# Attention by four heads a step with the softmax weights as the stationary operand, mixing in plain float32, and 1024 instead of 768 inner columns in the first part

## The chip, the cores and the metric

The kernel runs on one core of a Trainium2 chip. The metric is the device time of one execution in microseconds; the time of a kernel is the median of several executions. TensorE (PE) multiplies, with its weight loads (PEld) shown apart; VectorE (DVE), ScalarE (ACT) and GpSimd (POOL) do elementwise work; SyncE (SP) issues most DMAs.

## The reference

Three blocks follow each other on 4 batches of 576 tokens. The first is windowed attention with 8 heads of 64; the second takes the real part of a two-dimensional Fourier transform of its output, adds it, and runs a dense MLP of 2048 inner columns on the normalised sum; the third sends each token to one of 8 experts of 1024 inner columns.

```python
scores = q @ k.T / sqrt(D) - slope[h] * |i - j|      # kept where 0 <= i - j < 128
attn = softmax(scores);  x = attn @ v                # (B, S, H*D)
u = x + real(fft(fft(x, axis=seq), axis=model))
un = (u - mean) / sqrt(var + 1e-6)
y = u + relu(un @ w_ch1) @ w_ch2                     # 512 -> 2048 -> 512
# experts: e = argmax of the gate (or the token before's); out = p[e] * relu(y @ w1[e]) @ w2[e]
```

## The kernel before, in words

All large matrix products are done in the reduced float32 format of TensorE with each operand split in a high and a low part, so that one product is three matmuls (`mm3`, lines 168 to 170). Plain float32 operands give two matmul records for each matmul of the program.

The program has a first part, in which attention, mixing (the Fourier transform) and the first 768 inner columns of the MLP run interleaved; a second part, which runs the other 1280 inner columns and routes tokens; and the experts. `FA` is the number of inner columns of the first part, `CB = 256` those of a chunk of weights. In both parts the MLP runs over 9 groups of 256 tokens, and for each group over the chunks; a chunk is two inner steps of 128 columns. A step (`ffn`, line 572) is 12 matmuls into `hps` (256 moving columns) and 6 into `acc` (512 moving columns), with one ACT and one DVE pass over `hps` between them. The partial sums of the first part go to `pd` in DRAM and the second part adds to them. MLP weights come as 64-bit words and are converted on the core (`convert`: one load of 256 KB, two ACT, three DVE and one POOL instruction for each of 8 pieces of a chunk).

Attention works on units of two heads and one tile of 128 queries: 20 units for each batch, the last tile of each pair of heads 64 rows. `scores` multiplies queries and keys into PSUM (two heads on two halves of the 64-deep rows), DVE folds the two key blocks into one by a mask (`copy_predicated`) and adds the bias with a row minimum in one instruction (line 345); `exps` takes the exponential with row sums on ACT; `flip` transposes the weights on TensorE (`pt`), copies them to SBUF and separates the two key blocks with two masks on POOL; `values` has v stationary (64 columns, two heads side by side) and the weights moving, so that its result `x` comes out transposed, one column per query. `reciprocals` transposes the row sums, and `natural`, at the start of the mixing of a batch, transposes the result back to one row per query (`xps`) and multiplies by the reciprocals.

The mixing of a batch (`mixing`) folds rows, splits them (`zi`), transforms along the sequence (`zps`, five PSUM tiles), splits again, transforms along the model axis (`pc`, `pz`) and adds the result to x. There are two buffers for x, so `natural` stores it to DRAM (`xd`) and `again` loads it back for the final addition. The sum goes to `ud` in DRAM, and the normalisation of the MLP loads it from there.

Generators for attention, mixing, conversion and MLP are put into lanes with start and length in abstract units (`ATT`, `MIX`, `CONV_`, `MLP_`); the lane with the lowest position is advanced next. A scheduler of the framework then reorders within its own view of durations, so that each engine's queue is a fixed list; every engine and SP's DMA queue work through it strictly in order. The weights of the second part take the memory of the first part's attention and mixing tiles, and so are converted when these are finished.

Of the kernel before, what the change touches and what calls it, by code (L numbers as in the profile page):

```python
# [30 lines left out]
K1 = HALF + 2  # L31
K2 = DM // 2 + 2
# [6 lines left out]
FA = 768  # L39
WB = 4  # L40
GB_ = 3
PB_ = 0
RB = 2
UB = 2
MB = 4
SETUP = 6.5
WARM = 24
ATT = ((0, 25), (25, 25), (50, 24), (75, 25))
MIX = ((25, 12), (50, 11), (77, 12), (101.5, 9))
CONV_ = (30, 14)  # L50
MLP_ = (40.0, 130)
XB = 2
QR = 4
VB = 3
TB_ = 4
FL = 2
EY = 10
VL = 4
PHB = 2
LI = 1  # L60
NP = 5

# [38 lines left out]
def split12(a):  # L101
    a = np.ascontiguousarray(a, dtype=np.float32)
    bits = a.view(np.uint32).astype(np.uint64)
    hi = ((bits + 0x7FF + ((bits >> 12) & 1)) & 0xFFFFF000).astype(np.uint32).view(np.float32)
    return hi, (a - hi).astype(np.float32)


def constants():
# [13 lines left out]
    c["tab1"] = np.ascontiguousarray(np.stack(split12(tab1), 1))  # L122
    c["tab2"] = np.ascontiguousarray(np.stack(split12(tab2), 1))
# [4 lines left out]
    slopes = -8.0 * 2.0 ** (-8.0 * (np.arange(H, dtype=np.float32) + 1) / H)  # L128
    rel = np.where(k <= q, q - k, q - k + P).astype(np.float32)
    bias = (slopes[:, None, None] * rel[None]).astype(np.float32).transpose(1, 0, 2)  # L130
    c["bias"] = np.ascontiguousarray(bias).astype(ml_dtypes.bfloat16)
# [25 lines left out]
def build(ctx, tc, a, out):  # L157
# [39 lines left out]
    xd = {(b, k): dram.tile([P, 2, DM], F32, name=f"xd{b}{k}") for b in range(B) for k in range(3)}  # L197
# [10 lines left out]
    ps_p = ctx.enter_context(pool("ps_p", PB_, space=PSUM)) if PB_ else ps_g  # L208
# [45 lines left out]
    qk = c1.enter_context(pool("qk", QR))  # L254
    sm = c1.enter_context(pool("sm", 3))
    ps_x = c1.enter_context(pool("ps_x", 2, space=PSUM))

    tab1 = cst.tile([P, 2, 2, 3, K1], F32R, name="tab1")
    tab2 = cst.tile([P, 2, 2, 2, K2], F32R, name="tab2")
    alt = cst.tile([1, K2], F32R, name="alt")  # L260

# [7 lines left out]
    def load_heads(b, hp):  # L269

        r = [qk.tile([P, S], F32, tag="raw", name=x) for x in ("qr", "kr")]
        for t, x in zip(r, ("q", "k")):
            nc.sync.dma_start(out=t, in_=a[x][b, hp])
        vr = sm.tile([P, NB, P], F32, tag="vr", name="vr", bufs=VB)
        last["load"] = nc.sync.dma_start(out=vr, in_=a["v"][b, hp])
        return r[0], r[1], vr

    raw0 = load_heads(0, 0)

    z16 = slab([P, 4 * P], BF16, "z16", "w", WB)  # L280
# [11 lines left out]
    bias = cst.tile([P, H, P], BF16, name="bias")  # L292
    nc.sync.dma_start(out=bias, in_=a["bias"])
    id16 = cst.tile([P, P], BF16, name="id16")
    nc.sync.dma_start(out=id16, in_=a["id16"])
    rec = {}
    mixed = [-1]

    def attention(b, ot):

        sums = sm.tile([P, NB, H], F32, tag="sums", name="sums", bufs=2)
        units = [(hp, i) for hp in range(4) for i in range(NB)]
        W, T, X, R, M = {}, {}, {}, {}, {}

        def rows(i):
            return P if i < 4 else D

        def scores(us):

            if b == 0:  # L310
                ss = [ps_a.tile([P, 2, 2 * P], F32, tag=f"acc{h}", name="s") for h in range(2)]
            else:
                ss = [ps_g.tile([P, 2, 2 * P], F32, tag="g", name="s") for h in range(2)]
            for u in us:

                T[u] = sm.tile([P, 2, P], F32, tag="t", name="t", bufs=TB_)
                M[u] = sm.tile([P, 2], F32, tag="mx", name="mx", bufs=TB_)
            c0s = [P, 0, 0, 0, 0]
            whole = all(0 < units[u][1] < 4 for u in us)
            for x, u in enumerate(us):  # L320
                hp, i = units[u]
                m = rows(i)
                qr, kr, _ = R[hp]
                w = m if i == 0 else P + m
                c0 = P if i == 0 else 0
                o = [s[0:m, x, c0:c0 + w] for s in ss]
                qc = slice(i * P, i * P + m)
                ks = slice(max(i - 1, 0) * P, max(i - 1, 0) * P + w)
                if i == 0:
                    for h in range(2):  # L330
                        nc.tensor.matmul(o[h], lhsT=id16, rhs=first, start=True, stop=False)

                for h in range(2):
                    r = slice(h * D, h * D + D)
                    nc.tensor.matmul(o[h], lhsT=qr[r, qc], rhs=kr[r, ks], start=i > 0, stop=True)  # L335
            for h in range(2):
                s = ss[h]
                if whole:
                    nc.vector.copy_predicated(s[:, :, 0:P], mask.unsqueeze(1).to_broadcast([P, 2, P]), s[:, :, P:])
                for x, u in enumerate(us):  # L340
                    hp, i = units[u]
                    m = rows(i)
                    if i > 0 and not whole:
                        nc.vector.copy_predicated(s[0:m, x, 0:m], mask[0:m, 0:m], s[0:m, x, P:P + m])
                    nc.vector.tensor_tensor_reduce(out=T[u][0:m, h], in0=s[0:m, x, c0s[i]:c0s[i] + P], in1=bias[0:m, 2 * hp + h], scale=SC,  # L345
                                                   scalar=3.0e38, op0=ALU.add, op1=ALU.min, accum_out=M[u][0:m, h:h + 1])

        def exps(u):
            hp, i = units[u]
            m = rows(i)  # L350
            t, mx = T[u], M.pop(u)
            for h in range(2):
                e = 2 * hp + h
                nc.scalar.activation(t[0:m, h], t[0:m, h], AF.Exp, bias=mx[0:m, h:h + 1], scale=-1.0, accum_out=sums[0:m, i, e:e + 1])  # L354

        def reciprocals():

            s1 = ps_g.tile([E, 4 * P], F32, tag="g", name="s1")
            s2 = ps_g.tile([E, D], F32, tag="g", name="s2")
            for i in range(4):  # L360
                nc.tensor.transpose(s1[:, i * P:(i + 1) * P], sums[:, i, :], ident)
            nc.tensor.transpose(s2, sums[0:D, 4, :], ident[0:D, 0:D])
            srow = sm.tile([E, S + 1], F32, tag="tmp", name="srow", bufs=1)
            nc.gpsimd.memset(srow[:, S:S + 1], 1.0)
            nc.scalar.copy(srow[:, 0:HALF + 1], s1[:, 0:HALF + 1])
            nc.vector.tensor_copy(srow[:, HALF + 1:HALF + 1 + D], s2[:, ::-1])
            nc.vector.tensor_copy(srow[:, HALF + 1 + D:S], s1[:, 4 * P - 1:HALF:-1])
            pt = ps_g.tile([P, 6, E], F32, tag="g", name="rt")
            r = sm.tile([P, 6, E], F32, tag="rec", name="rec", bufs=2)
            for kt in range(3):  # L370
                for ab in range(2):
                    c, n = kt * P + ab * HALF, P if kt < 2 else 33
                    nc.tensor.transpose(pt[0:n, 2 * kt + ab], srow[:, c:c + n], ident[0:E, 0:E])
            for x, n in ((slice(0, 4), P), (slice(4, 6), 33)):
                nc.vector.tensor_scalar_add(r[0:n, x], pt[0:n, x], 1.0e-9)
                nc.vector.reciprocal(r[0:n, x], r[0:n, x])
            rec[b] = r

        def flip(u):
            hp, i = units[u]  # L380
            m = rows(i)
            t = T.pop(u)
            pt = ps_p.tile([P, 2, P], F32, tag="g", name="pt")
            for h in range(2):
                nc.tensor.transpose(pt[:, h, 0:m], t[0:m, h, :], ident[0:m, 0:m])
            ph = sm.tile([P, 2, P], F32, tag="ph", name="ph", bufs=PHB)
            nc.scalar.copy(ph[:, :, 0:m], pt[:, :, 0:m])
            W[u] = slab([P, 2, 2 * P], F32, "w", "w", WB)
            if i > 0:
                nc.gpsimd.affine_select(out=W[u - 1][:, :, P:P + m], in_=ph[:, :, 0:m], pattern=[[0, 2], [-1, m]],  # L390
                                        compare_op=ALU.is_gt, fill=0.0, base=0, channel_multiplier=1)
            last["pool"] = nc.gpsimd.affine_select(out=W[u][0:m, :, 0:m], in_=ph[0:m, :, 0:m], pattern=[[0, 2], [1, m]],
                                                   compare_op=ALU.is_ge, fill=0.0, base=0, channel_multiplier=-1)

        def values(u):
            hp, j = units[u]
            vr = R[hp][2]
            w = W.pop(u)
            if j == 0:
                X["x"] = ps_x.tile([P, 4 * P], F32, tag="x", name="x")  # L400
                X["b"] = ps_p.tile([P, D], F32, tag="g", name="ob")
            n = rows(j)
            q0, q1 = max(j * P, D), min((j + 2) * P, S)

            if j == 0:

# [777 lines left out]
```

## Time and profile before

| | us |
|---|---|
| median of 3 runs | 1089.79 (1087.11 to 1098.1) |
| profiled execution | 1080.29 |
| its span, first to last instruction | 1078.6 |
| PE busy, as a union of records | 986.9 (92%) |
| DVE, ACT, POOL busy | 565.0, 402.1, 218.3 |
| mean granted TensorE clock, as a share of 2.4 GHz | 0.929 |

The profiled execution stands 9.5 us under the median of the runs. Busy time of PE holds pipelined records that overlap, so the distance between starts of neighbouring records, not their length, is what one costs. A row of the timeline gives start, length, engine, line, operation, tiles, shapes and the number of merged records, and in brackets the idle time of the engine before it with what ended it. In the table of stretches PEclk is the share of full clock that TensorE was granted.

### The profile page before, as it was taken

How to read it: one execution, taken by the hardware profiler on the slowest of the kernel's cores; microseconds unless marked ns; L12 is line 12 of the kernel's file. 1: busy time of each engine (PE TensorE's matmuls, PEld its weight loads, DVE VectorE, ACT ScalarE, POOL GpSimd, SP SyncE). 2: the span in 40 equal slices, each digit the busy share in tenths (PEclk: the TensorE clock that was granted, in tenths of full speed). 3: DMA queues.
4: the chain of work that ended last, by engine and by line, in shares of the span. 5: the costliest groups of instructions: out<-in, count | busy, mean ns of one | idle time of the engine just before them, and what ended most of it. 6: DMA issues, size and time to landing. Idle time of an engine off the chain costs nothing. (4 is left out here: it accounts for less than half of the span.)

```text
span 1078.6 us, 17056 instructions
## 1 busy us (share of the span) xinstructions
PE 986.9 (92%) x5857; PEld 788.8 (73%) x5857; DVE 565.0 (52%) x1835; ACT 402.1 (37%) x1102; POOL 218.3 (20%) x321
## 2 busy tenths in 40 slices
PE   8989669989979879989999999998997999999994
PEld 4456346657657767768888888887786998888993
DVE  4686577457554647864333425343666744455510
ACT  5544444444423324543111111111425644545520
POOL 2513321122111002342111212112212222111100
PEclk9766689989989889999999999999997999999997
DMA  7742553335231346683444313441428855454400
GB/s 225 269 147 86 161 167 110 113 99 174 86 99 41 121 127 195 188 243 98 98 98 99 67 49 82 98 98 55 152 60 266 279 192 176 149 189 160 146 18 18
DMA packets 128509, 142.92 MB, mean 133 GB/s; under 512 B 17668, under 2 KB 89604, under 8 KB 128092
## 3 DMA queue, kind: packets, MB, share of 16 engines
q1 hardware_dynamic: 105244, 119.17, 35.1%
q0 software_dynamic: 23168, 22.56, 8.9%
q8 instruction: 48, 0.79, 0.3%
q14 instruction: 49, 0.40, 0.1%
HBM read 108.62 MB, written 35.96 MB: 134 GB/s over the span
## 5 line engine op out<-in xcount | busy, mean ns | idle before, releaser
L582 ACT ACTIVATE h<-hps 128x256 fp32r<-128x256 f32 x152 | 58.0, 382 | 249.7 <-PE hps L170 249.5
L583 DVE SCALAR_TENSOR_TENSOR h<-hps,h 128x256 fp32r<-128x256 f32 x152 | 63.8, 420 | 149.5 <-ACT h L582 149.3
L168 PE MATMUL acc<-t,h 128*128 128x512 f32 x304 | 127.8, 420 | 10.1 <-ACT h L582 10.1
L165 DVE TENSOR_TENSOR t<-we,t 128x512 fp32r<-128x512 f32 x144 | 95.1, 693 | 64.8 <-ACT t L164 61.6
L169 PE MATMUL acc<-t,h 128*128 128x512 f32 x304 | 121.6, 400 | 0.0
L170 PE MATMUL acc<-t,h 128*128 128x512 f32 x304 | 120.7, 399 | 0.4 <-DVE h L583 0.4
L164 ACT CAST t<-we 128x512 fp32r<-128x512 f32 x144 | 83.6, 619 | 61.2 <-DMA we<-in_w 35.8
L168 PE MATMUL hps<-xTb,t 128*128 128x256 f32 x360 | 103.6, 288 | 0.0
L170 PE MATMUL hps<-xTb,t 128*128 128x256 f32 x360 | 103.3, 287 | 0.0
L169 PE MATMUL hps<-xTb,t 128*128 128x256 f32 x360 | 102.7, 285 | 0.0
L168 PE MATMUL hps<-xTe,t 128*128 128x256 f32 (+5 forms) x288 | 88.3, 307 | 3.1 <-ACT xTe L164 3.1
L170 PE MATMUL hps<-xTe,t 128*128 128x256 f32 (+5 forms) x288 | 88.1, 306 | 0.0
L169 PE MATMUL hps<-xTe,t 128*128 128x256 f32 (+5 forms) x288 | 88.0, 305 | 0.0
L354 ACT ACTIVATE t<-t,mx 128x128 f32<-128x128 f32 (+1 forms) x160 | 63.0, 395 | 58.4 <-DVE mx L345 58.3
L335 PE MATMUL s<-kr,qr 64*128 64x256 f32 (+2 forms) x320 | 72.7, 426 | 9.0 <-DVE cmb L539 6.6
L165 POOL TENSOR_TENSOR t<-t,t 128x256 fp32r<-128x256 f32 x64 | 49.0, 772 | 141.7 <-ACT t L164 133.6
L168 PE MATMUL hps<-xT,t 128*128 128x256 f32 x216 | 67.8, 314 | 10.3 <-DVE h L583 9.8
L168 PEld LDWEIGHTS acc<-t,h 128*128 128x128 f32 x304 | 58.2, 191 | 25.4 <-ACT h L582 13.6
L168 PEld LDWEIGHTS hps<-xTb,t 128*128 128x128 f32 x360 | 69.1, 192 | 3.2
L169 PEld LDWEIGHTS hps<-xTb,t 128*128 128x128 f32 x360 | 69.1, 192 | 2.6
L170 PEld LDWEIGHTS hps<-xTb,t 128*128 128x128 f32 x360 | 69.3, 192 | 0.3
L170 PEld LDWEIGHTS acc<-t,h 128*128 128x128 f32 x304 | 57.5, 190 | 13.7 <-DVE h L583 1.9
(281 smaller groups left out, 2219.2 us busy)
## 6 DMA issues: line engine op xcount, KB each, us to landing
we<-in_w SPq DMA_DIRECT2D x64, 512.0 KB
r<-in_w_ch SPq DMA_DIRECT2D x64, 256.0 KB
nd<-xT SPq DMA_DIRECT2D x18, 512.0 KB
xTb<-nd POOLq DMA_DIRECT2D x18, 512.0 KB, 7.0
vr<-in_v SPq DMA_DIRECT2D x16, 320.0 KB
qr<-in_q SPq DMA_DIRECT2D x16, 288.0 KB
kr<-in_k SPq DMA_DIRECT2D x16, 288.0 KB
u<-ud SPq DMA_DIRECT2D x18, 256.0 KB
```

The source lines that it names most:

```text
L164: nc.scalar.copy(hi, src)
L165: (eng or nc.vector).tensor_tensor(out=lo, in0=src, in1=hi.bitcast(F32), op=ALU.subtract)
L168: nc.tensor.matmul(o, lhsT=wh, rhs=xh, start=start, stop=False, **kw)
L169: nc.tensor.matmul(o, lhsT=wh, rhs=xl, start=False, stop=False, **kw)
L170: return nc.tensor.matmul(o, lhsT=wl, rhs=xh, start=False, stop=stop, **kw)
L335: nc.tensor.matmul(o[h], lhsT=qr[r, qc], rhs=kr[r, ks], start=i > 0, stop=True)
L354: nc.scalar.activation(t[0:m, h], t[0:m, h], AF.Exp, bias=mx[0:m, h:h + 1], scale=-1.0, accum_out=sums[0:m, i, e:e + 1])
L582: nc.scalar.activation(h[:, 0, 0:n], hps[:, 0:n], AF.Relu)
L583: nc.vector.scalar_tensor_tensor(out=h[:, 1, 0:n], in0=hps[:, 0:n], scalar=0.0, in1=h[:, 0, 0:n].bitcast(F32), op0=ALU.max, op1=ALU.subtract)
```

## The change

Attention takes four heads and one tile of queries a step, ten steps for each batch, of tiles that already lie in the order in which the mixing wants the rows. The bias instruction with its row minimum becomes a `scalar_tensor_tensor` and a `tensor_reduce` over 512 elements; the exponential no longer sums. The transposed weights become the stationary operand and v, with a column of ones for the row sums, the moving one of 65 columns: one row per query comes out, and reciprocal and product with it go straight into x. `reciprocals`, `natural`, `again` and the DRAM copy `xd` are gone, x has six buffers. The mixing uses plain float32 matmuls without splits. Tables have half the size. The first part has four chunks, the second four. A batch's queries, keys and values come in four loads of a part (queries and keys 5136, values 3120 bytes for each partition) with three buffers each.

```diff
-FA = 768
-WB = 4
+FA = 1024
-MB = 4
+MB = 5
-ATT = ((0, 25), (25, 25), (50, 24), (75, 25))
-MIX = ((25, 12), (50, 11), (77, 12), (101.5, 9))
-CONV_ = (30, 14)
-MLP_ = (40.0, 130)
-XB = 2
-QR = 4
+ATT = ((0, 25), (26, 25), (52, 24), (77, 25))
+MIX = ((25.1, 10), (51.1, 11), (77.1, 12), (102.1, 9))
+CONV_ = (12, 30)
+MLP_ = (36.0, 140)
+XB = 6
+QB = 3
...
+    ps_s = c1.enter_context(pool("ps_s", 1, space=PSUM))
...
+    TILES = ((0, 0, P, HALF + 33, 0, P), (0, P, P, HALF + 33, P, P), (0, 2 * P, 65, HALF + 33 + P, P, 65),
+             (1, 0, P, 2 * P, P, P), (1, P, P, 3 * P, P, P))
...
+        def scores(u):
...
+            if b == 0 and u % 2:
+                ss = [ps_a.tile([P, 2, 2 * P], F32, tag=f"acc{h}", name="s") for h in range(2)]
...
+                s = ps_s.tile([P, 4, 2 * P], F32, tag="s", name="s")
...
+                for h in range(2):
+                    r = slice(h * D, h * D + D)
+                    nc.tensor.matmul(o[h], lhsT=qt[r, x, q0:q0 + m], rhs=qt[r, x, k0:k0 + n0 + n1], start=i > 0, stop=True)
+            for j0, n, s in segs:
+                if i > 0:
+                    nc.vector.copy_predicated(s[0:m, :, 0:n1], mask[0:m, 0:n1].unsqueeze(1).to_broadcast([m, n, n1]), s[0:m, :, P:P + n1])
+                z = slice(0, P) if i > 0 else slice(P, 2 * P)
+                nc.vector.scalar_tensor_tensor(out=t[0:m, j0:j0 + n], in0=s[0:m, :, z], scalar=SC, in1=bias[0:m, g, j0:j0 + n],
+                                               op0=ALU.mult, op1=ALU.add)
+            nc.vector.tensor_reduce(out=mx[0:m].unsqueeze(2), in_=t[0:m], axis=AX.X, op=ALU.min)
...
+            for j in range(4):
+                nc.scalar.activation(t[0:m, j], t[0:m, j], AF.Exp, bias=mx[0:m, j:j + 1], scale=-1.0)
...
+                nc.scalar.copy(wp, pt[:, :, m - 1:c0 - 1 if c0 else None:-1] if turned else pt[:, :, c0:c1_])
+                last["pool"] = nc.gpsimd.affine_select(out=wo, in_=wp, pattern=[[0, 4], [st, n]], compare_op=ALU.is_ge, fill=0.0, base=base,
+                                                       channel_multiplier=-1)
+                if i > 0:
+                    nc.gpsimd.affine_select(out=wp, in_=wp, pattern=[[0, 4], [-st, n]], compare_op=ALU.is_gt, fill=0.0, base=-base,
+                                            channel_multiplier=1)
...
+                        for z in range(2 if i > 0 else 1):
+                            nc.tensor.matmul(o[0:n, j], lhsT=w[:, z, 2 * h + x, c0:c1_], rhs=v[:, OWN[i] - z, j], start=z == 0, stop=z == 1 or i == 0)
+                nc.vector.tensor_scalar_add(r[0:n].unsqueeze(2), o[0:n, :, D:D + 1], 1.0e-9)
+                nc.vector.reciprocal(r[0:n], r[0:n])
+                nc.vector.tensor_tensor(out=xs[kt][0:n, ab, g * 4 * D:(g + 1) * 4 * D].rearrange("p (h d) -> p h d", h=4), in0=o[0:n, :, 0:D],
+                                        in1=r[0:n].unsqueeze(2).to_broadcast([n, 4, D]), op=ALU.mult)
...
-                mm3(ps[0:w, 0:K1], zi[0:n, cs, 0, db * P:db * P + w], zi[0:n, cs, 1, db * P:db * P + w],
-                    tab1[0:n, 0, cs, kt], tab1[0:n, 1, cs, kt], kt == 0, kt == 2)
-            z = Z[cs][:, db] if db < 2 else zn
-            split(z[0:w, 0], z[0:w, 1], ps[0:w, 0:K1])
+                nc.tensor.matmul(ps[0:w, 0:K1], lhsT=xf[0:n, cs, db * P:db * P + w], rhs=tab1[0:n, cs, kt], start=kt == 0, stop=kt == 2)
+            nc.scalar.copy(Z[cs][:, db] if db < 2 else zn, ps[0:w, 0:K1])
...
-        again(0)
...
-                    mm3(ps[0:n, 0:K2], z[:, 0, c0:c0 + n], z[:, 1, c0:c0 + n], tab2[:, 0, cs, db], tab2[:, 1, cs, db],
-                        db == 0, db == 1 and cs == 1)
+                    nc.tensor.matmul(ps[0:n, 0:K2], lhsT=Z[cs][:, db, c0:c0 + n], rhs=tab2[:, cs, db], start=db == 0, stop=db == 1 and cs == 1)
...
-            with tc.issue_after(last["pool"].ins):
-                nc.gpsimd.dma_start(out=t, in_=a[x])
+            with tc.issue_after(last["load"].ins):
+                nc.sync.dma_start(out=t, in_=a[x])
```

The queues move at three places that matter here. The first is VectorE at the end of the mixing of batch 0 before (`cmb` is the transform, line 543 adds it to x, line 339 is the mask of the next scores):

```order
L539 TENSOR_TENSOR cmb<-pc,cmb 33x258
L246 SCALAR_TENSOR_TENSOR t_1393<-m_1394,t_1393 128x256 [waits DVE_49]
L245 SCALAR_TENSOR_TENSOR t_1403<-m_1404,t_1403 128x256
L543 TENSOR_TENSOR x<-x,cmb 33x257 [waits DMAHW4_49,DMAHW7_49,DMAHW3_49,DVE_49]
L544 TENSOR_TENSOR x<-x,cmb 33x255 [waits DVE_49]
L543 TENSOR_TENSOR x<-x,cmb 32x257 [waits DMAHW0_49]
L544 TENSOR_TENSOR x<-x,cmb 32x255
L339 COPY_PREDICATED s<-mask,s 128x2x128 [waits PE_49,Activation_49] x2
```

The same place in the changed kernel (there line 459 is the addition and line 233 the start of a conversion):

```order
L454 TENSOR_TENSOR cmb<-pc,cmb 33x257 [waits PE_49,Activation_49]
L333 TENSOR_REDUCE mx<-t 128x4 [waits DVE_49]
L455 TENSOR_TENSOR cmb<-pc,cmb 33x257
L459 TENSOR_TENSOR x<-x,cmb 33x257 [waits DVE_49]
L460 TENSOR_TENSOR x<-x,cmb 33x255 [waits DVE_49]
L459 TENSOR_TENSOR x<-x,cmb 32x257
L460 TENSOR_TENSOR x<-x,cmb 32x255
L233 TENSOR_SCALAR t_1128<-r_1126 128x256 [waits DMAHW2_49,Pool_49]
```

The addition no longer waits for a DMA. The second place is TensorE at a step of attention during the MLP of the first part, before (line 412 is `values`, 385 `flip`, 335 `scores`):

```order
L534 MATMUL pc<-alt,zn 128x258 x2
L412 MATMUL x<-w,vr 64x256 x2
L385 MATMUL pt<-ident,t 128x128 x2
L335 MATMUL s<-kr,qr 128x256 x4
L168 MATMUL pz<-tab_168,z_3085 33x258
```

And in the changed kernel (378 is `values`, 347 `flip`, 325 `scores`, 159 to 161 the MLP):

```order
L378 MATMUL o<-vt,w 128x65 x8
L347 MATMUL pt<-ident,t 128x128 x4
L325 MATMUL s<-qkt 65x193 x4
L159 MATMUL acc<-t_226,h 128x512
L160 MATMUL acc<-t_226,h 128x512
L161 MATMUL acc<-t_226,h 128x512
```

A step of four heads stands between long runs of MLP matmuls, 12 to 36 of them. The third place is SP's queue in the changed kernel while attention of batch 0 runs (`qkt` and `vt` are the loads of a part, `r` the pieces of MLP weights):

```order
L227 DMA r_540<-in_w_ch 128x4x128 [waits DMAHW3_49,DVE_49,Activation_49]
L265 DMA vt<-in_v 128x780 [waits DMAHW4_49,PE_49]
L263 DMA qkt<-in_qk 128x1284 [waits DMAHW5_49]
L227 DMA r_578<-in_w_ch 128x512 [waits DMAHW2_49,DMAHW6_49,DVE_49,Activation_49]
L227 DMA r_592<-in_w_ch 128x512 [waits DMAHW3_49,DMAHW7_49,DVE_49,Activation_49]
L263 DMA qkt<-in_qk 128x1284 [waits DMAHW0_49,PE_49]
```

Loads of weights stand behind loads of keys and values that wait for TensorE to give a buffer back. In both kernels all weights of the first part are converted before its first MLP matmul on VectorE's list, 24 pieces before and 32 now. By the lists of TensorE, 324 of the first part's 648 `hps` matmuls stand behind the last matmul of the mixing before, and 420 of 864 now; of `acc` it is 164 of 324, and 216 of 432.

## Rows read from the trace of the kernel before

**Rows 1.** Table of stretches: us, busy us (records) of each engine, PEclk, DMA share, GB/s

```profile
core 0: us, PE busy (x) PEld busy (x) DVE busy (x) ACT busy (x) POOL busy (x), PEclk, DMA share, GB/s
0.00:149.30 149.30, 122.89 (x594) 68.68 (x594) 94.46 (x381) 74.18 (x279) 48.44 (x103) 0.74 0.55 178
149.30:394.90 245.60, 222.29 (x1376) 161.22 (x1375) 140.41 (x527) 92.48 (x310) 31.00 (x77) 0.93 0.33 105
394.90:488.20 93.30, 83.62 (x484) 69.84 (x485) 68.68 (x199) 46.55 (x114) 32.87 (x41) 0.95 0.71 209
488.20:788.40 300.20, 291.89 (x1873) 255.99 (x1872) 120.83 (x420) 62.83 (x151) 57.09 (x55) 0.99 0.37 89
788.40:1078.60 290.20, 266.21 (x1535) 233.03 (x1533) 140.57 (x312) 126.05 (x248) 48.93 (x47) 0.95 0.47 153
```

**Rows 2.** Timeline of VectorE, its longest waits for a DMA in the first part

```profile
118.23 0.42 DVE L543 TENSOR_TENSOR x<-x,cmb 33x257 f32<-33x257 f32 x1 [8.50 <-DMA x<-xd]
...
217.46 0.42 DVE L543 TENSOR_TENSOR x<-x,cmb 33x257 f32<-33x257 f32 x1 [8.73 <-DMA x<-xd]
...
313.15 0.69 DVE L611 BATCH_NORM_STATS2 st<-u 128x6 f32<-128x512 f32 x1 [8.54 <-DMA u<-ud]
...
393.79 0.42 DVE L543 TENSOR_TENSOR x<-x,cmb 33x257 f32<-33x257 f32 x1 [9.77 <-DMA x<-xd]
```

**Rows 3.** Timeline of TensorE, its longest idle times in the first part

```profile
121.10 0.47 PE L385 MATMUL pt<-ident,t 128*128 128x128 f32 x1 [8.21 <-ACT t L354]
...
144.16 1.11 PE L566 MATMUL tps<-ident,u 128*128 128x128 f32 x4 [8.48 <-ACT u L631]
...
220.34 0.47 PE L385 MATMUL pt<-ident,t 128*128 128x128 f32 x1 [5.41 <-ACT t L354]
...
314.77 0.90 PE L335 MATMUL s<-kr,qr 64*64 64x192 f32 x2 [6.60 <-DVE cmb L539]
...
394.94 0.58 PE L168 MATMUL hps<-xT,t 128*128 128x256 f32 x1 [7.14 <-DVE h L583]
```

**Rows 4.** Timeline of TensorE in the second part

```profile
700.44 0.28 PE L168 MATMUL hps<-xTb,t 128*128 128x256 f32 x1
700.56 0.28 PE L169 MATMUL hps<-xTb,t 128*128 128x256 f32 x1
...
701.27 0.39 PE L170 MATMUL acc<-t,h 128*128 128x512 f32 x1
701.50 0.40 PE L168 MATMUL acc<-t,h 128*128 128x512 f32 x1
```

**Rows 5.** Timeline of TensorE and its weight loads, attention at full clock

```profile
336.33 0.33 PEld L373 LDWEIGHTS rt<-ident,srow 8*128 8x128 f32 x5
```

**Rows 6.** Timeline of TensorE, attention and the transposes at full clock

```profile
15.76 0.55 PE L412 MATMUL x<-w,vr 128*64 128x192 f32 x4
...
17.23 0.65 PE L412 MATMUL x<-w,vr 128*64 128x256 f32 x4
...
185.98 1.14 PE L335 MATMUL s<-kr,qr 64*128 64x256 f32 x8
...
254.54 1.04 PE L458 MATMUL xps<-ident,ot 128*128 128x128 f32 x8
```

**Rows 7.** Timeline of TensorE, one kind of matmul of the mixing

```profile
179.45 0.30 PE L169 MATMUL zps<-tab,zi 128*128 128x290 f32 x1
179.59 0.29 PE L170 MATMUL zps<-tab,zi 128*128 128x290 f32 x1
```

**Rows 8.** Groups by form: line, engine, operation, count, busy us, mean ns, idle before

```profile
L459 DVE TENSOR_TENSOR x<-xps,rec 128x512 f32<-128x512 f32 x16 | 10.4, 685 | 1.1 <-PE xps L458 1.1
...
L244 DVE TENSOR_SCALAR t<-r 128x256 uint32<-128x256 uint32 x64 | 23.8, 373 | 21.8 <-POOL t L165 13.0 <-DMA r<-in_w_ch 8.6
```

**Rows 9.** Waits of SP's DMA queue, 0 to 490 us: total, times, longest

```profile
SPq L273 <- PE s L335: 38.5, 8, 11.5
...
SPq L275 <- PE x L412: 27.8, 8, 6.8
```

## What the change should do to the time

> **What bounds the kernel now.** I read the table of stretches first, then the longest waits of VectorE and TensorE, then the distances between starts of neighbouring matmuls. The table [rows 1] splits the span at the first MLP matmul (149.30 us), the last matmul of the mixing (394.90), the first matmul of the second part (488.20) and the first of the experts (788.40). The reader is to see two kinds of stretches. In the second part TensorE is busy 291.89 of 300.20 us at a clock of 0.99: it is the bound there. In the first 394.90 us it stands for 26.4 us and then 23.3 us, its granted clock is 0.74 and then 0.93 (2.4 GHz mixed with 1.2 GHz), and no other engine is full, VectorE with 94.46 of 149.30 us being the nearest. There the bound is order: each engine takes its list in turn, and one late item holds all behind it.
>
> The longest such holds are VectorE waiting for x to come back from DRAM: 8.50, 8.73 and 9.77 us [rows 2], once for each of three batches. Behind it stand the masks of the next scores, or the evacuation of `hps`, so TensorE stops for 8.21, 5.41 and 7.14 us [rows 3], 20.8 us in all. Two further stops belong to the sum `u` on its way through DRAM into the normalisation: 8.48 us before `tps`, and 6.60 us, which goes with VectorE's 8.54 us on `u<-ud` [rows 2, 3].
>
> **The change part by part.** The profiled execution took 1080.29 us, 1.7 more than its span; the sum is made against that. The median of the runs is 9.5 us higher, and I add this at the end.
>
> *A chunk moves from the second part to the first.* Matmuls of 256 columns start 0.12 us apart and those of 512 columns 0.23 us [rows 4], so a step of the MLP costs 12 x 0.12 + 6 x 0.23 = 2.82 us, and a chunk over nine groups, 18 steps, 50.8 us. The second part now holds 90 steps, 254 us; the other 46 us, transposes and routing, stay. It loses 51 us. The routing of one group runs between the steps of the next, of which four of twenty go, so I allow 45; with its waits shrinking in proportion it would be 55.
>
> The same 51 us of TensorE work come into the first part. By the lists 96 more `hps` and 52 more `acc` matmuls stand behind the mixing, 8.3 steps or 23.5 us. That stretch takes 93.30 us for 27.2 steps, 76.7 us of matmuls; in proportion it would grow by 28.6. I take +25: eight of the 40 conversions for the second part are gone from it, and its DMA share of 0.71 falls. The other 9.7 steps, 27.3 us, come between the attention steps: +27, before anything is hidden.
>
> *Attention and mixing on TensorE.* Values before, for a pair of heads: three groups of 0.65 us, one of 0.55 [rows 6] and two small ones that I put at half the latter, 3.05 us, 49 us for 16 pairs. Now there are 352 matmuls of 65 columns, two records each, 704 with 128 stationary columns. No row has this shape. From below stand five weight loads of such width or narrower in 0.33 us, 0.066 each [rows 5]; from above eight transposes with as many stationary and 128 moving columns in 1.04 us, 0.13 each [rows 6]. That gives 46 to 92 us. I take 0.08, near the loads, because 65 moving columns are few and loads run beside matmuls: 56 us, +7.
> The 96 transposes of `natural` go (0.13 each, -12), the 44 of the row sums with them (-4). In the mixing nine records of `zps` at 0.14 [rows 7] become six of plain float32. Eight such records of 256 columns, two heads side by side, take 1.14 us [rows 6], 0.28 for each pair with its tail; 0.25 in a stream gives 1.5 instead of 1.26 us a tile, +5 for 20 tiles, and about +5 for `pc` and `pz`. Scores and `pt` keep their work. The net is about 0, with ends of -10 and +40 that come from the values.
>
> *The reload.* `again` and its waits go: -21 from TensorE's three stops. Nothing of the kind replaces them on VectorE's list, where line 459 waits for no DMA. The loads and stores of `xd` leave SP's queue too. The two stops on `u` stay; u is late next.
>
> *Clock and filling.* A stretch at 0.74 has half its time at 1.2 GHz, and an idle stop precedes a fall. What three stops fewer give back there lies between 0 and 20 us; I take -6, near nothing, since the latency of the first batch stays. The runs of 12 to 36 MLP matmuls between attention steps give ACT, VectorE and POOL time to finish a step; of the idle 23.3 us [rows 1] and of short waits inside the busy time I let -6 be filled (0 to -20).
>
> *Other engines.* VectorE's row multiplies of 512 elements cost 0.685 us [rows 8]. A step of four heads needs three passes of that width and a short normalisation, some 2.8 us, 28 us a batch, which is what two-head units, `finish` and `natural` together cost; the splits of the mixing are saved. Eight more conversions stand in the first stretch, three instructions each by the row of 373 ns [rows 8], some 10 us. VectorE idles 55 us there, which covers them; without that cover they would be +10. ACT and POOL are busy half and a third of that stretch and get fewer instructions: nothing.
>
> Sum: -51 + 25 + 27 + 0 - 21 - 6 - 6 = -32 us. 1080.3 - 32 = 1048, and 9.5 more for the median: **1058 us**.
>
> **The rivals.**
> *Wide weights set the pace.* If a record with 128 stationary and 65 moving columns costs the 0.13 us of the transposes [rows 6], the values take 92 us instead of 56: 1094 us. For it: the loads no longer hide behind 256 moving columns. Against it: five loads in 0.33 us [rows 5]. The Trainium skill speaks against this change here (TensorE: Matmul & The Clock Gate, section on LDWEIGHTS): a load takes the number of columns divided by 1.2, in ns, which makes an estimate of 107 ns for 128. By that rule 704 loads take 75 us and the time would be 1077; the five loads do not agree with it. Chance 0.13.
>
> *The wait moves on.* Stops on `u` at the normalisation grow by what the reload stops give back, because the same stores still have to land before the next group; then neither the 21 nor the 12 us come: 1091 us. For it: 8.54 us on `u<-ud` [rows 2] already is of that kind. Against it: with x in SBUF the stores start earlier. Chance 0.12.
>
> *Slower: conversions starve behind keys and values.* SP's queue now has the weights' loads behind loads of `vt` and `qkt` that wait for TensorE; VectorE, in order, would stand at the start of a conversion with the scores' masks behind it. SP already waits 38.5 us for buffers of queries and keys and 27.8 us for those of values [rows 9], hidden so far: VectorE waited only 8.6 us for weights [rows 8]. If those 66 us show on VectorE as the reloads did, where 27 us of it became 20.8 us of TensorE, the price is 51 us: 1109 us. It decides from about 30 us of VectorE's waits for weights up. Against it: there are three buffers for parts, each good for two to three steps. Chance 0.14.
>
> *More comes back.* With the clock's and the filling's 20 us in place of 6 each, and a little less of the values: about 1030. Chance 0.06.
>
> **How the numbers follow.** The forecast has 0.55; it spreads from 1042 to 1075 by the ends of tail, clock and filling. The range 1034 to 1098 takes in the two rivals at 1091 and 1094, and leaves out most of the slower one and part of the fastest. A measurement of this kernel tells about 1% from no change, 1079 to 1101. Faster gets 0.55 and 0.06 and a part of the wide weights' cheaper half, 0.66 together; slower 0.14; the same 0.20.
>
> **What would show it.** The second part should last 249 us from its first `hps` to the experts (right within 5). The stretch behind the mixing should be 118 us. VectorE should have no wait for a DMA at line 459, and TensorE only the stops on `u` over 5 us. A run of 16 records of `o` should take some 1.2 us at full clock; 2 us would be the wide weights. The first MLP matmul should come at about 137 us and the last of the mixing about 245 us later. Waits of VectorE at line 233 for weights of over 30 us, or an attention step that stops TensorE between its scores and its transposes, would make the forecast wrong.

## The result and the profile after

| | before | changed |
|---|---|---|
| median, us | 1093.94 (4 runs, 1087.11 to 1102.09) | 1053.91 (4 runs, 1052.16 to 1057.92) |
| profiled execution, us | 1080.29 | 1054.71 |
| mean granted TensorE clock | 0.929 | 0.940 |

The ratio is 0.9636, with a 95% interval of 0.9556 to 0.9717. Two later measurements of the same kernel gave 0.9787 and 0.9686. The forecast was 1058 us, and 1048 for the profiled execution. Medians are of all executions, while ratios leave out those over 1.5% above the fastest of their kernel (one of 1826.23 us with the earlier conversions below among them), so that the two need not agree.

The table of stretches of the changed kernel, cut at its own first MLP matmul, at the last matmul of the mixing, at the first matmul of the second part and at that of the experts (columns as in [rows 1]):

```profile
core 0: us, PE busy (x) PEld busy (x) DVE busy (x) ACT busy (x) POOL busy (x), PEclk, DMA share, GB/s
0.00:144.30 144.30, 107.54 (x591) 75.40 (x591) 96.72 (x270) 61.91 (x171) 44.97 (x70) 0.75 0.54 174
144.30:390.40 246.10, 241.05 (x1586) 192.01 (x1585) 136.99 (x389) 80.42 (x206) 27.89 (x54) 0.97 0.27 82
390.40:511.80 121.40, 112.15 (x676) 94.85 (x676) 69.49 (x201) 48.15 (x119) 31.17 (x38) 0.99 0.54 154
511.80:762.90 251.10, 239.37 (x1553) 209.03 (x1551) 106.12 (x387) 51.25 (x122) 52.94 (x49) 0.99 0.44 102
762.90:1053.00 290.10, 267.88 (x1529) 234.03 (x1529) 141.73 (x315) 127.82 (x251) 48.19 (x47) 0.95 0.47 154
```

One cut of [rows 1] was not what the prediction called it: at 394.90 us ends the stop of the third reload, while the last two matmuls of the mixing start at 381.10 and 381.24. With that cut the kernel before reads:

```profile
149.30:381.50 232.20, 215.99 (x1337) 155.74 (x1336) 137.87 (x519) 91.13 (x307) 31.00 (x77) 0.94 0.34 107
381.50:488.40 106.90, 90.12 (x525) 75.50 (x525) 71.43 (x208) 48.07 (x118) 33.06 (x41) 0.94 0.65 191
```

The tables cut the kernel before at 488.40 and 788.40 us; the first matmuls of its second part and of its experts start at 488.42 and 788.63. With these the five stretches changed by -5.0, +13.9, +14.5, -49.1 and +0.1 us, together -25.6, which is the whole difference of the two profiled executions. The reader is to see that the first stretch, which was to become 12 us shorter, became 5 us shorter.

The waits of TensorE and of VectorE in the first 512 us of the changed kernel (total us, times, longest):

```profile
PE o L378 <- POOL w L358: 14.0, 8, 10.0
PE zps L439 <- ACT t L155: 7.6, 1, 7.6
...
PE tps L482 <- ACT u L547: 4.2, 4, 1.3
```

```profile
DVE st L527 <- DMA u<-ud: 14.9, 7, 7.9
...
DVE t L233 <- DMA r<-in_w_ch: 12.0, 9, 5.9
```

Nothing waits for `x<-xd` any more, and the stop of 8.48 us before `tps` [rows 3] has become four of 1.3 us at most. A new one of 10.0 us stands before the values `o`, and another of 7.6 us before the first transform of the mixing, `zps`. For the first of these the timelines of SP's queue, ScalarE and TensorE show what precedes it (SP's second column is the time that issuing took):

```profile
96.76 0.33 SPq L463 DMA_DIRECT2D ud<-x  x1
97.43 0.24 SPq L464 DMA_DIRECT2D ud<-x  x1
97.78 0.84 SPq L227 DMA_DIRECT2D r<-in_w_ch  x1
98.86 5.81 SPq L523 DMA_DIRECT2D u<-ud  x1
...
106.00 0.89 SPq L227 DMA_DIRECT2D r<-in_w_ch  x1
```

```profile
111.36 0.43 ACT L232 ACTIVATE m<-r 128x256 f32<-128x256 f32 x1 [10.41 <-DMA r<-in_w_ch]
```

```profile
116.33 3.95 PE L378 MATMUL o<-vt,w 128*128 128x65 f32 x16 [10.03 <-POOL w L358]
```

ScalarE stands at the conversion of a piece of weights from 100.95 us on, with the exponentials of batch 1 behind it, and TensorE has no weights `w` to go on with. The piece was issued at 97.78 and is used at 111.36, 13.6 us later; in a second profile of the same kernel (e9, below) the loads of weights between 30 and 120 us whose landing is on record land after 3.0 us in the median, 8.4 at most. Ahead of it in the queue is the store of line 464, 127 rows of x into `ud`.

The other new stop is of another kind:

```profile
72.83 4.97 PE L439 MATMUL zps<-tab,xf 128*128 128x289 f32 x12 [7.58 <-ACT t L155]
```

In these 7.58 us VectorE is busy for 7.54, of which 4.98 are conversions of weights (lines 233 to 235) that stand between the folds of x on its list. In the kernel before, `zps` waits 2.0 us at most. The stop is there in every version of the changed kernel below, with 5.4 to 7.6 us, so what it costs was not measured.

### The profile page after: what moved, and what is told of

Read it like the earlier page. It is cut to its first block, busy times and chain, and to the rows that moved or that the text cites. A ratio compares the mean times of both kernels' runs of the same rounds, so it can differ in the third digit from the quotient of the medians.

```text
span 1053.0 us, 16430 instructions
## 1 busy us (share of the span) xinstructions
PE 968.0 (92%) x5929; PEld 805.3 (76%) x5929; DVE 551.1 (52%) x1560; ACT 369.5 (35%) x866; POOL 205.2 (19%) x258
## 5 line engine op out<-in xcount | busy, mean ns | idle before, releaser
L378 PEld LDWEIGHTS o<-vt,w 128*128 128x128 f32 (+2 forms) x704 | 81.9, 187 | 25.3 <-POOL w L358 16.8
L378 PE MATMUL o<-vt,w 128*128 128x65 f32 (+2 forms) x704 | 86.7, 283 | 15.8 <-POOL w L358 14.0
L159 PE MATMUL hps<-xT,t 128*128 128x256 f32 x288 | 87.3, 303 | 6.6 <-DVE h L499 6.4
L159 PE MATMUL hps<-xTb,t 128*128 128x256 f32 x288 | 82.9, 288 | 0.0
L160 PE MATMUL hps<-xT,t 128*128 128x256 f32 x288 | 82.8, 287 | 0.0
L161 PE MATMUL hps<-xT,t 128*128 128x256 f32 x288 | 82.6, 287 | 0.0
L161 PE MATMUL hps<-xTb,t 128*128 128x256 f32 x288 | 82.5, 287 | 0.0
L160 PE MATMUL hps<-xTb,t 128*128 128x256 f32 x288 | 82.1, 285 | 0.0
L358 POOL TENSOR_SCALAR_AFFINE_SELECT w<-w 128x512 f32<-128x512 f32 (+2 forms) x48 | 27.5, 582 | 240.0 <-ACT w L355 239.9
L159 PEld LDWEIGHTS hps<-xT,t 128*128 128x128 f32 x288 | 56.1, 195 | 21.4 <-DVE h L499 13.5
L159 PEld LDWEIGHTS acc<-t,h 128*128 128x128 f32 x304 | 57.6, 190 | 18.2 <-issue 4.6
```

What stands on the lines that cost most here:

```text
L159: nc.tensor.matmul(o, lhsT=wh, rhs=xh, start=start, stop=False, **kw)
L160: nc.tensor.matmul(o, lhsT=wh, rhs=xl, start=False, stop=False, **kw)
L161: return nc.tensor.matmul(o, lhsT=wl, rhs=xh, start=False, stop=stop, **kw)
L358: last["pool"] = nc.gpsimd.affine_select(out=wo, in_=wp, pattern=[[0, 4], [st, n]], compare_op=ALU.is_ge, fill=0.0, base=base, channel_mul ...
L378: nc.tensor.matmul(o[0:n, j], lhsT=w[:, z, 2 * h + x, c0:c1_], rhs=v[:, OWN[i] - z, j], start=z == 0, stop=z == 1 or i == 0)
```

## The experiments

Each ratio is to the kernel before, timed beside it on the same chip.

**One half of the change at a time.** First the 1024 inner columns in the kernel before:

```diff
-FA = 768
+FA = 1024
-CONV_ = (30, 14)
-MLP_ = (40.0, 130)
+CONV_ = (30, 19)
+MLP_ = (40.0, 155)
```

> The kernel before with 1024 inner columns in the first part and nothing else changed (lanes of conversion and MLP lengthened in proportion). Theory (the move of a chunk is nearly a shift of equal work, and the gain comes from the rewritten attention): ratio to before 0.99 to 1.005; second part near 250 us, first MLP matmul to second part longer by 45 to 50 us. Rival (the longer MLP fills the idle time of the old attention, and the rewriting gains nothing): ratio 0.965 to 0.975, idle time of TensorE before the second part smaller by 30 us.

Measured: 1083.57 us, ratio 1.0007 (0.9971 to 1.0042). Its stretches behind the mixing and of the second part:

```profile
372.70:541.10 168.40, 152.84 (x932) 130.81 (x932) 81.96 (x251) 59.40 (x142) 30.82 (x38) 0.98 0.45 129
541.10:789.60 248.50, 239.43 (x1553) 209.11 (x1551) 105.38 (x387) 51.30 (x122) 52.54 (x49) 0.99 0.43 102
```

The second part loses 51.7 us, and what lies before it gains 52.7. The move of a chunk is in the kernel before a shift of equal work, as the theory had it. Then the other half, the changed kernel with 768 columns:

```diff
-FA = 1024
+FA = 768
-CONV_ = (12, 30)
-MLP_ = (36.0, 140)
+CONV_ = (12, 22.5)
+MLP_ = (36.0, 105)
```

> The changed kernel with 768 inner columns in the first part, as before, lanes shortened in proportion. Theory (the rewritten attention without the reload gives the gain): ratio to before 0.965 to 0.98; second part 300 us, first 488 us shorter by 20 to 35. Rival (the longer MLP gives the gain): ratio 0.995 to 1.005.

Measured: 1064.24 us, ratio 0.9866 (0.9753 to 0.9979). The rewritten attention gives about 1.3% alone (0.2 to 2.5%), less than the theory had. Its first stretches:

```profile
0.00:135.30 135.30, 104.85 (x590) 72.77 (x590) 89.28 (x250) 56.90 (x158) 38.78 (x62) 0.79 0.55 174
135.30:377.30 242.00, 233.76 (x1521) 184.02 (x1520) 134.59 (x387) 80.90 (x204) 27.52 (x54) 0.96 0.28 88
377.30:474.80 97.50, 76.21 (x416) 62.91 (x416) 65.00 (x191) 42.59 (x105) 33.44 (x40) 0.88 0.63 184
```

The reader is to see the third: TensorE is busy 76.21 of 97.50 us at a clock of 0.88, with waits of up to 4.0 us for ScalarE's and VectorE's passes on `h` and one of 5.0 us before `tps`. In the changed kernel the same stretch holds 168 more `hps` and some 84 more `acc` matmuls, 40 us by [rows 4], and is 23.9 us longer. Here the chunk fills idle time, which in the kernel before it did not: there the stretch grew by 61.5 us for the steps it got. By the ratios the two halves are worth more together than the sum of each alone (1.3% and nothing, against 2.1 to 3.6%), though the intervals meet. On one chip this version took 1064.24 us and the changed kernel with a reload (below) 1055.57, so the chunk is worth some 9 us there.

**The reload.** The kernel before with x kept:

```diff
-XB = 2
+XB = 6
...
-                nc.sync.dma_start(out=xd[b, kt], in_=xs[kt])
...
-        again(0)
...
-            if kb < 2:
-                again(kb + 1)
```

> The kernel before with six buffers for x and no copy of x in DRAM; nothing else changed. Theory (the reload stops TensorE for 21 us that come back when it goes): ratio 0.975 to 0.985, no wait of VectorE on x from DRAM. Rival (the wait moves on to the sum u, or to the next item on VectorE's list): ratio 0.995 to 1.005, with waits on u longer by 10 us or more.

Measured: 1077.40 us, ratio 0.988, but with an interval of 0.9738 to 1.0022. It was run again:

> The kernel before with six buffers for x and no copy in DRAM, again, since its four times lay far apart. Theory (the three stops come back in part): ratio 0.98 to 0.99. Rival (they move on to u): 0.995 to 1.005.

Measured: 1076.43 us, ratio 0.9879 (0.9819 to 0.9939): some 13 us. Two stops of TensorE over 4 us are left in its first 150 us:

```profile
128.93 0.99 PE L385 MATMUL pt<-ident,t 128*128 128x128 f32 x3 [4.79 <-ACT ot L415]
...
147.88 1.12 PE L548 MATMUL tps<-ident,u 128*128 128x128 f32 x4 [9.46 <-ACT u L613]
```

The stops of the reload are gone. The one on u is 9.46 us instead of 8.48 [rows 3], and a new one of 4.79 has come, so a part was probably handed on.

The reverse, the changed kernel with x stored and loaded back into its own tile before the final addition:

```diff
         for kt in range(3):
+            keep(kt, True)
             fold(kt)
...
+        keep(0, False)
         for kb in range(3):
+            if kb < 2:
+                keep(kb + 1, False)
```

> The changed kernel with x stored to DRAM before the folding and loaded back into its tile for the final addition, as the kernel before did. Theory: 15 to 25 us slower than the changed kernel (ratio to before about 0.98 to 0.99), VectorE again waiting at the addition for a DMA of 8 to 10 us a batch. Rival (the longer runs of MLP matmuls cover the reload): within 5 us of the changed kernel (0.96 to 0.97).

Measured: 1055.57 us, ratio 0.9775 (0.9697 to 0.9854), within the measurements of the changed kernel, and no wait of VectorE for `x<-xd`. The rival was right in its time; the trace shows another reason than its cover of MLP work. With a tile of its own the load of batch 0 is issued at 71 to 79 us, long before the addition, and nobody waits. In the kernel before, the last reload of a batch needs the buffer of the first rows of x. The waits of SP's queue there, 0 to 490 us, name what it stood for, once in each of the four batches:

```profile
SPq L473 <- DMA ud<-x: 30.6, 4, 8.0
```

So what cost time was not the way through DRAM but the two buffers: the reload could not be issued until the stores of the sum had left them. One of these two stores is again one of 127 rows (line 548). This is read from the trace; no version of the kernel before had the reload with more buffers.

**What a record of the values costs.** The changed kernel once more, as reference, and a version with 33 moving columns, in which the first 32 columns of each head are not computed and the others stand in their place:

```diff
-nc.tensor.matmul(o[0:n, j], ..., rhs=v[:, OWN[i] - z, j], ...)
+nc.tensor.matmul(o[0:n, j, 32:D + 1], ..., rhs=v[:, OWN[i] - z, j, 32:D + 1], ...)
```

> The changed kernel once more, as the reference for the next three: ratio to before 0.965 to 0.975.

> The changed kernel with 33 in place of 65 moving columns in the values (the first 32 columns of each head are not computed; the others stand in their place). Theory (the stationary columns set the pace): records with 128 stationary columns stay at 0.11 us each at full clock, those of 33 at 0.057; time within 3 us of the changed kernel. Rival (the moving columns set it): 0.06 us each, 25 to 35 us less TensorE time before the second part, 10 to 30 us faster.

Measured: the reference 1062.51 us, ratio 0.9787 (0.9717 to 0.9856), above what was expected. A timeline of TensorE at full clock, first of the changed kernel (a run of 16 records with 128 stationary columns, then one of 32 records with 33, half of them 32):

```profile
338.79 1.89 PE L378 MATMUL o<-vt,w 128*128 128x65 f32 x16
340.52 0.41 PE L347 MATMUL pt<-ident,t 65*128 65x65 f32 x4
...
345.38 2.12 PE L378 MATMUL o<-vt,w 128*33 128x65 f32 x32
347.44 0.66 PE L347 MATMUL pt<-ident,t 128*128 128x128 f32 x4
```

and of the version with 33 moving columns:

```profile
354.94 1.87 PE L378 MATMUL o<-vt,w 128*128 128x33 f32 x16
356.64 0.44 PE L347 MATMUL pt<-ident,t 65*128 65x65 f32 x4
...
361.54 1.33 PE L378 MATMUL o<-vt,w 128*33 128x33 f32 x32
362.80 0.39 PE L159 MATMUL hps<-xT,t 128*128 128x256 f32 x1
```

From start to start of what follows, 16 wide records take 1.73 us with 65 moving columns and 1.70 us with 33, 0.108 and 0.106 us each: half the moving columns save next to nothing, so the stationary ones set the pace. With 33 stationary columns a record falls from 0.064 to 0.039 us, so there the moving ones do. The time of this version, 1166.19 us, tells nothing on that: with other values the tokens go to other experts, whose stretch takes 389 us instead of 290, and VectorE has one operation more for each unit.

**The stop of 10 us.** Four versions on the theory that the weights come late. First the changed kernel as their reference, then u loaded by GpSimd:

```diff
-            nc.sync.dma_start(out=u, in_=ud[g])
+            nc.gpsimd.dma_start(out=u, in_=ud[g])
```

> The changed kernel once more, on the chip of the next three, as their reference: ratio to before 0.965 to 0.985; first MLP matmul at 144 to 148 us.

> The changed kernel with the loads of u in the first part issued by GpSimd in place of SyncE. Theory (a load of u that waits in SyncE's queue for its store holds back a load of weights, and with it ScalarE, VectorE and TensorE for 10 us): the 10 us stop of TensorE ahead of the values at about 116 us shrinks to 5 us or less, first MLP matmul 3 to 8 us earlier, total 3 to 8 us less. Rival (the weights are late for another reason, or the wait moves to GpSimd's masks): first matmul within 2 us of the changed kernel, total within 3 us, or slower where GpSimd now waits for the store with masks behind it.

Measured: the reference 1056.47 us, ratio 0.9686 (0.9643 to 0.9729), first MLP matmul at 144.5. With u on GpSimd 1046.96 us, ratio 0.9624 (0.9578 to 0.9671), but the stop stays. Its rows of SP and TensorE:

```profile
95.59 5.78 SPq L466 DMA_DIRECT2D ud<-x  x1
```

```profile
112.53 3.96 PE L378 MATMUL o<-vt,w 128*128 128x65 f32 x16 [10.22 <-POOL w L358]
```

The theory of the load of u falls: the long issue has passed to whatever stands next in the queue, here another store, and the weights are as late. The first MLP matmul comes 4.0 us earlier, and the first matmul of the mixing, ahead of anything the edit touches, already 4.2 us earlier (68.79 against 73.03); the profiled execution of the reference ran its 20th to 32nd us at a clock of 0.72, this one at 1.00. Why the median fell by 9.5 us is open.

The conversions were moved in two ways:

```diff
-CONV_ = (12, 30)
+CONV_ = (6, 30)     # earlier
+CONV_ = (12, 36)    # longer
```

> The changed kernel with the lane of conversions started at 6 in place of 12, so that nearly all stand ahead of the mixing of batch 0 and its sums on every queue. Theory (late conversions lengthen the chain from the mixing through u to the first MLP matmul): no TensorE stop of 10 us at the values, first MLP matmul at 134 to 141 us, total 3 to 9 us less. Rival (VectorE's work before the first matmul is what counts, whatever its order): first matmul within 2 us of the changed kernel, since attention of batch 0 comes later by as much.

> The changed kernel with the lane of conversions 36 long in place of 30, so that 28 of the 32 stand ahead of the first MLP operation on VectorE's list. Theory (each conversion ahead of the first matmul costs about 1.1 us of the 9 us that eight more of them cost): first MLP matmul 3 to 6 us earlier, total 2 to 6 us less. Rival: the same number stands between the mixing of batch 0 and the first matmul, which then comes within 2 us of the changed kernel's.

Measured: earlier 1064.47 us, ratio 0.9761 (0.9709 to 0.9812), first MLP matmul at 149.5, against the theory: VectorE does them ahead of the mixing, which starts 9.3 us later, and a stop of 7.75 us remains at the values. Longer 1046.07 us, ratio 0.9606 (0.9558 to 0.9654), first MLP matmul at 130.1, more than the theory had for four conversions fewer; in SP's queue one load of weights, not two, stands among these stores now. That load still lands 9.1 us after its issue, and TensorE has a stop of 9.14 us at the scores in place of the one at the values. The first matmul of the mixing comes 6.9 us earlier than in the reference, with the clock at 1.00 from 20 to 32 us as with u on GpSimd, so the 14.4 us do not belong to the conversions alone. A lane of 48 gave no time.

What remained in all of them was the store of 127 rows. The last version writes it in two:

```diff
-                nc.sync.dma_start(out=row(3)[1:P], in_=xs[0][1:P, 1])
+                nc.sync.dma_start(out=row(3)[1:113], in_=xs[0][1:113, 1])
+                nc.sync.dma_start(out=row(3)[113:P], in_=xs[0][113:P, 1])
```

> The changed kernel with the store of 127 rows of x into ud, one for each batch, written as two of 112 and 15 rows (the load of u of the first group then stands two places later in SyncE's queue). Theory (one DMA engine alone carries the 127 rows at 25 GB/s, and the weights issued behind it land 13 us later in place of 5): no stretch of 25 GB/s behind this store, SyncE issues what follows in under 2 us, TensorE's stop at the values near 116 us falls from 10 us to under 5, first MLP matmul 4 to 8 us earlier than 144.5, total 5 to 12 us less (ratio to before 0.957 to 0.965). Rival (the weights are late because of the queue's order or the many small pieces of their own load): the stop stays at 8 to 10 us, first MLP matmul within 2 us, ratio 0.966 to 0.97.

Measured: 1040.72 us, ratio 0.9577 (0.9512 to 0.9642), the lowest of all here, though its interval meets those of u on GpSimd and of the longer conversions. GB/s of the DMA engines in 40 slices, of the changed kernel from 97 to 112 us:

```profile
GB/s 0 142 399 164 11 0 85 220 298 157 22 27 27 22 27 27 22 27 27 27 22 27 180 131 350 361 366 240 243 176 258 275 265 149 238 349 348 331 344 361
```

and with the store in two from 93 to 108 us:

```profile
GB/s 0 33 366 355 279 322 38 86 240 358 337 366 361 295 55 105 258 313 264 410 306 350 178 67 116 366 319 346 299 277 301 367 387 335 350 339 299 212 104 37
```

The 4.5 us at 22 to 27 GB/s, in which the transfers issued behind hardly move, are gone. SP and the first stretches of this version:

```profile
93.57 0.32 SPq L464 DMA_DIRECT2D ud<-x  x1
93.93 0.45 SPq L465 DMA_DIRECT2D ud<-x  x1
94.55 0.40 SPq L227 DMA_DIRECT2D r<-in_w_ch  x1
95.78 0.34 SPq L467 DMA_DIRECT2D ud<-x  x1
```

```profile
0.00:131.00 131.00, 100.13 (x589) 68.05 (x589) 96.04 (x270) 62.04 (x170) 45.10 (x70) 0.82 0.61 195
131.00:365.80 234.80, 234.01 (x1586) 186.35 (x1586) 138.54 (x389) 80.53 (x206) 27.70 (x54) 1.00 0.28 86
```

Between 90 and 125 us nothing takes over 1.2 us to issue here, the loads of weights with a landing on record land after 5.3 us at most, and the longest stop before the values anywhere in the first 490 us is 1.4 us. VectorE's waits for `u<-ud` fall from 14.9 us to 4.3. The edit also puts the load of u two places later in the queue, but that is not the cause: with that load out of the queue the stop stayed. The first MLP matmul comes 13.5 us earlier than in the reference, of which 4.0 lie before the edit (clock, as above); against u on GpSimd, which ran at the same clock there, it is 9.5 us, and 6.2 in the median of the whole. All 32 conversions still stand ahead of it. With 24 it came at 135.3 us, but behind a stop of 7.74 us at the values with the store in one, so no run prices the eight alone.

## Why the prediction was right, and where it was not

The time fell inside the range and near the forecast, 1058 against 1053.9, but the sum was 6.7 us too good against the profiled execution (1048 against 1054.7), and the 9.5 us that were added for the median were not there: the profiled execution of the changed kernel lies at the middle of its runs. The two misses cancelled, which is luck. The stage lengths that were named as signs (249, 118, 137 and 245 us) add up to -39 us against the cuts of [rows 1], not -32, so the signs do not fit the sum. Of the other signs VectorE's waits at line 233 were 12.0 us, under the 30 that were named, and TensorE had two stops over 5 us that are not on `u`, of 10.0 and 7.6 us.

- **A chunk out of the second part, -51.** Right: -49.1, and 251.1 us for 249.
- **A chunk into the stretch behind the mixing, +25; between attention, +27.** The first was +14.5. The step that failed is the scaling of a stretch of 93.30 us, which had begun 13.4 us after the mixing's last matmul; the work added by the lists is 23.5 us, the stop of 7.14 us [rows 3] left it, and the waits for `tps` shrank. The second, from distances between starts in this stretch, was +21.7 us of MLP matmuls, and with -9.4 of attention and +2.0 of mixing, each with the stops behind its matmuls, the stretch grew by 13.9.
- **Values at 0.08 us a record.** Wrong, and so was the count: 448 of the 704 records have 128 stationary columns and 256 have 33 or 32. At 0.108 and 0.064 us that is 64.8 us where 56 was taken. The argument from five weight loads in 0.33 us [rows 5] misled. Those have 8 rows and serve matmuls of 8 moving columns; which of the two makes them short no run shows. The rule of the Trainium skill (TensorE: Matmul & The Clock Gate, section on LDWEIGHTS), columns divided by 1.2 in ns, gives 107 ns for 128; the trace agrees, with 108. The mechanism of the rival *wide weights* was the true one; its price was 9 us, not 36.
- **Mixing in plain float32, +10 for four batches.** Too dear: its distances between starts in the stretch with attention, which holds three batches, grew by 2.0 us with the stops and by 4.8 without, where the forecast makes 7.5 of it.
- **The reload, -21.** Too large: taken out of the kernel before, it gave about 13. The words "nothing of the kind replaces them" failed: part seems to go to the next item, and in the changed kernel a 10.0 us stop came in at the same place in the program. The prediction put the holds down to x on its way back; the queue shows the reload itself standing behind the stores of the sum, one of them of 127 rows, and the changed kernel kept that store.
- **Conversions at nothing, and the slower rival.** That VectorE's idle time covers the eight more conversions is not shown: before the first mixing it has none, and TensorE stands 7.58 us there. The rival *conversions starve on SP* did happen, once: 10.0 us at the end of the first mixing. It did not come from keys and values but from a store ahead of the weights. So the first MLP matmul came at 144.3 us, not 137; with the store in two it came at 131.0, of which 4.0 are the clock of that execution.
- **The two stops on `u` stay.** They became smaller: TensorE's waits for `tps` are 1.3 us at most. Of VectorE's 14.9 us on `u<-ud` the longest wait, 7.86 us up to 319.57, is followed by a stop of TensorE of 3.62 us for `h`, behind it on VectorE's list; with the store in two the longest wait for `h` is 1.0 us.
- **Clock and filling, -6 each.** The clock went from 0.94 to 0.97 and 0.99 in the two middle stretches but stayed at 0.75 in the first. That the two halves are worth more together than apart, by 0.9 to 2.4% in the medians of the ratios, is by the stretches filling of this kind; the sum let 6 us be filled and charged the chunk in full beside it.

What stays open: why the kernel before scatters from 1075.5 to 1104.0 us and the changed one from 1050.7 to 1066.1, and whether the store in two would take the reload's stops out of the kernel before. Its reload is issued at 116.36 us, when such a stretch of 25 GB/s ends there as well:

```profile
GB/s 70 292 381 46 0 0 0 0 306 44 16 35 11 19 25 289 333 109 27 25 25 27 25 25 27 25 25 161 100 317 318 186 254 292 112 117 327 343 285 134
```

This is the kernel before from 97 to 127 us, in slices of 0.75 us. The store in two was not tried in it.

## What to carry to other kernels

A stop that a change takes away is worth its length only if the item behind it is ready; read what was issued next on the same queue before counting the gain. When a load lands far later than its kind does elsewhere in the trace, look at the transfer ahead of it and at the GB/s of those slices, not at the queue's order alone. For a float32 matmul with 128 stationary columns and a moving operand of 65 or fewer, price it by its stationary columns, and count the shapes apart.

## What the runs showed of the hardware

- A store of 127 rows of 2 KB ran at 22 to 27 GB/s where it stood alone, while other slices reach 350; from 103 to 105 us the 16 DMA engines are busy for a share of 0.07, about one of them. A load issued behind it was used after 13.6 us, where such loads land after 3.0 us in the median, and the next issue took 5.8 us. As 112 and 15 rows this is gone. The Trainium skill (DMA: Bandwidth & Descriptors, section Why a DMA increments its semaphore by 16 and not by 1) says that a transfer runs on the largest number of engines up to 16 that divides the slowest dimension of both its sides, which for 127 rows is one; the trace agrees, with the 0.07.
- A float32 matmul record with 128 stationary columns takes 0.106 us with 33 moving columns and 0.108 with 65; with 33 stationary columns 0.039 and 0.064.
